# Between two MoE layers: where VectorE, ScalarE and TensorE each take a piece of the hand-over, in a three-stage attention and MoE kernel

## The chip, the cores and the metric

The kernel runs on one core of one Trainium2 chip. A time is the device time of that core in microseconds (us), from the first to the last instruction with what lies around it; of a kernel the median over several runs is given. A profile is of one further execution.

## What is computed

Attention over 4 batches, 8 heads, 768 positions and width 64, with a local window, a few global keys and a bias by distance; its output is read as 3072 tokens of width 512. Then two mixtures of eight experts (512 to 1024 to 512), the second on the output of the first:

```python
def _moe_ref(x, w_gate, w_output_gate, w1, w2):
    logits = x @ w_gate
    e_idx = np.argmax(logits, axis=1)
    ...
    for e in range(E):
        mask = e_idx == e
        h = np.maximum(x[mask] @ w1[e], 0.0)
        ye = h @ w2[e]
        out[mask] = gate_w[mask, None] * eom[mask, e, None] * ye

def _moe2_ref(x, w_gate, w1, w2):
    cap = N // E
    logits = x @ w_gate
    order = np.argsort(-logits.flatten())
    # greedy: each token goes to its best expert that has room, cap = 384 tokens each
    ...
    for e in range(E):
        mask = assigned == e
        h = np.maximum(x[mask] @ w1[e], 0.0)
        out[mask] = h @ w2[e]
```

The second assignment depends on all logits at once, so it can't begin before the first MoE has given the logits of every token.

## The kernel before

**Products in two parts.** Each fp32 matrix is split into a high part (the value rounded by ScalarE, names ending in h: wah, wbh, xh, hh) and a low part (the value less the high part: wal, wbl, xl, hl), and each product is three matmuls. `weight_chunk` (line 113) does this for a weight: a load of 512 KB into `raw` on the SP queue (three buffers, and one more for the last chunk later on), the high part on ScalarE (L119), the low part by a subtraction (L121) on the engine that `lo_engine` names, in one instruction or in two halves; `load_w1` and `load_w2` call it for the four chunks of a matrix. Layer 1 of an expert is at L175 with its evictions at L179 (ScalarE) and L180 (VectorE), layer 2 at L207, or L191 in transposed form.

**Two MoEs.** The loop over eight expert positions of the first MoE runs position e's layer 1 and layer 2 in turn, but of the last two (6 and 7) it runs layer 1 alone. Their logits for the second MoE are taken from the hidden rows at once (`gate_early` at L935, copied by ScalarE at L788 out of `lp` into a tile of name yo, turned by TensorE at L792, reduced by VectorE at L794, scattered by GpSimd at L86). So all logits are in DRAM before the last two layer 2 have run; the load of `L` (L1364, SP) collects them. Position 7's second matrix is loaded into the tag "wa", as soon as layer 1 of position 7 has read that tag for the last time.

**The second MoE** assigns one expert at a time: `phase(i, ...)` finds the expert that fills next by picking digits of the sorting key (six rounds; in each VectorE compares at L1123, TensorE counts at L1134, VectorE copies at L1136, TensorE folds at L1141, VectorE compares at L1144, TensorE spreads at L1150, VectorE takes the digit at L1152). Then L1216 and L1225 name the expert (`ei`, on which SP waits to load its first matrix, tag "wb"), L1229 to L1241 place its tokens (`cs`, `spx`, and the copy `csb` at L1234), and 24 matmuls at L1281 give their row numbers (`idx`, L1283 and L1285). GpSimd gathers these rows (L1321) into XB, TensorE turns them (L151), and the expert's layers follow.

**What sets the order.** TensorE's order is written out by `merge(ffns(), [phases(), weights(), tokens()])`: each matmul of the layers yields its modelled duration in ns (a 512-column one 213), each step of a phase yields how long to let the layers run before its next step, and `merge` interleaves them by these numbers. `ffns` begins with layer 2 of positions 6 and 7 (192 matmuls at L207, with `out1` as what is done with each of their eight row blocks, L946 and a scatter at L86); only phase 0 runs beside them, the phases from 1 on wait for their end. Phase 0 begins after 10000 ns of them. The other engines' orders come from a scheduler that simulates the program. Each engine works through its order strictly, so a wait holds everything behind it.

Of the kernel before, what the change touches and what calls it, by code (L numbers as in the profile page):

```python
# [14 lines left out]
AF = mybir.ActivationFunctionType  # L15
OP = mybir.AluOpType
# [13 lines left out]
def attention_moe_moe_kernel(  # L30
# [17 lines left out]
    nc = tc.nc  # L48
# [36 lines left out]
    def scatter(kind, dst, idx, src):  # L85
        st = nc.gpsimd.indirect_dma_start(  # L86
            out=dst, out_offset=bass.IndirectOffsetOnAxis(ap=idx, axis=0), in_=src, in_offset=None)
        indep(kind, st)
        return st
# [23 lines left out]
    def weight_chunk(src, tag, i, nfree, lo_engine, raw_view, halves=False):  # L113
        rp, nb_ = (raw_pools[-1], 1) if i == 3 and len(raw_pools) > 1 else (raw_pools[0], 3)
        raw = rp.tile([128, nfree], F32, tag="raw", name="raw", bufs=nb_)
        nc.sync.dma_start(raw if raw_view is None else raw.rearrange(raw_view[0], **raw_view[1]), src)
        hi = wpool.tile([128, nfree], F32R, tag=f"{tag}h{i}", name=f"{tag}h{i}")
        lo = wpool.tile([128, nfree], F32R, tag=f"{tag}l{i}", name=f"{tag}l{i}")
        nc.scalar.activation(hi, raw, AF.Copy)  # L119
        for c in (slice(0, nfree // 2), slice(nfree // 2, nfree)) if halves else (slice(0, nfree),):  # L120
            lo_engine.tensor_tensor(lo[:, c], raw[:, c], hi[:, c], op=OP.subtract)  # L121
        return hi, lo

    def load_w1(src, tag="wa", lo=(nc.gpsimd,), ks=range(KD), halves=False):
        return [weight_chunk(src[kk], tag, kk, FF, lo[kk % len(lo)], None, halves) for kk in ks]

    def load_w2(src, tag="wb", ks=range(KF // 2), lo_engine=nc.gpsimd, halves=False):
        r = []
        for i in ks:
            hi, lo = weight_chunk(src[i], tag, i, 2 * DM, lo_engine, ("p (c d) -> p c d", dict(c=2)), halves)  # L130
            for c in range(2):
                r.append((hi[:, c * DM:(c + 1) * DM], lo[:, c * DM:(c + 1) * DM]))
        return r
# [122 lines left out]
    with ExitStack() as actx:  # L256
# [68 lines left out]
        if not dense:  # L325
# [11 lines left out]
            if n_global:  # L337
                nc.vector.memset(dist[:, G0:G0 + n_global], float(n_local))
                nc.vector.tensor_scalar(dist[:, 256:256 + n_global], dist[:, 256:256 + n_global], float(n_local), None,
                                        op0=OP.min)  # L340
# [361 lines left out]
    def merge(main, sides):  # L702


        sides = [[s, 0.0] for s in sides]
        for cost in main:
            dt = max(0.0, min(w for _, w in sides)) if cost is None else cost
            for s in list(sides):
                s[1] -= dt
                while s[1] <= 0:  # L710
                    w = next(s[0], None)
                    if w is None:
                        sides.remove(s)
                        break
                    s[1] = w
        for s, _ in sides:
            for _ in s:
                pass
# [14 lines left out]
    def expert(i):  # L733

        if i not in who:
            who[i] = nc.sync.value_load(order[0:1, i:i + 1], min_val=0, max_val=E - 1)
        return who[i]

    def w1_of(i):
        return [w1[ds(expert(i), 1), kk * 128:(kk + 1) * 128].rearrange("o p f -> (o p) f") for kk in range(KD)]  # L740

    def w2_of(i):
        return [w2[ds(expert(i), 1), c * 256:(c + 1) * 256].rearrange("o (c p) d -> p (o c) d", p=128)
                for c in range(KF // 2)]
# [25 lines left out]
    with ExitStack() as bctx:  # L770
# [168 lines left out]
        def out1(e):  # L939
            sc, ii = aux[e]  # L940
            bt = PLAN[e][1]

            def done(j, yp):
                y = yb.tile([128, DM], F32, name="yo")[0:bt]
                with tc.high_priority():
                    nc.vector.tensor_scalar(y, yp, sc[:, j:j + 1], None, op0=OP.mult)  # L946
                    scatter("x2", x2d, ii[:, j:j + 1], y)
            return done

        last_load = [load_x(0)]  # L950
        last = [None]
# [14 lines left out]
        wa, wb = pre[0], pre[1]  # L966
# [3 lines left out]
        for e in range(E):  # L970
            hs = []
            nb, bt = PLAN[e]
            n_ = nb * bt
            l1 = layer1(wa, xt, n_, hs, e in (0 if dense else E, E - 1))
            mparts = [chain(*[gate_part(*p) for p in parts[e]])]
            if e == E - 2:
                merge(l1, mparts)
                lp = ps.tile([128, 512], F32, name="lp", tag="sp")[:, 0:n_]
                rest = chain(l2, gate_early(e, hs, mfs[e], lp))
            else:  # L980
                merge(l1, back + (mparts if e == E - 3 else []))
            if e + 1 < E:
                wa = load_w1(w1_of(e + 1), lo=(nc.gpsimd, nc.vector))
                xt = new_xt()

            def transposes(xt=xt, e=e, step=1500):
                for j in range(PLAN[e + 1][0]):
                    transpose_block(xt, XB[0:PLAN[e + 1][1], j], j, PLAN[e + 1][1])
                    yield step
                keep_aux(e + 1)  # L990

            if e < E - 2:
                yt = new_yt()
                l2 = layer2t(wb, hs, n_, yt)
                merge(islice(l2, 3 * KF * (KD - 1)) if e == E - 3 else l2, [transposes()] + (mparts if e < E - 3 else []))
                back = [rows_back(e, yt)]
                last_load[0] = load_x(e + 2)
                if e < E - 3:
                    wb = load_w2(w2_of(e + 1))
            elif e == E - 2:  # L1000
                merge(rest, [transposes(step=1200)])
                back.append(gate_scatter(lp, nb, bt, *aux[e], wait=5000))
                wb = load_w2(w2_of(e))
                hs_last.append((hs, wb))
            else:
                lp = ps.tile([128, 512], F32, name="lp", tag="sp")[:, 0:n_]
                for _ in gate_early(e, hs, mfs[e], lp):
                    pass
                for _ in gate_scatter(lp, nb, bt, *aux[e]):
                    pass  # L1010
                with tc.issue_after(last[0].ins):
                    wb = load_w2(w2_of(e), tag="wa")
                hs_last.append((hs, wb))


# [64 lines left out]
    def phase(i, found):  # L1080

        last = i == E - 1
# [15 lines left out]
        else:  # L1098
# [8 lines left out]
            y = sel.tile([128, 6, NC_], F32, name="yk")  # L1107
# [96 lines left out]
            for i_ in range(2):  # L1204
# [4 lines left out]
                                           op0=OP.is_ge, op1=OP.mult)  # L1209
# [14 lines left out]
        ei = sel.tile([128, 1], I32, name="ei", bufs=E)  # L1224
        nc.vector.tensor_scalar(ei, mx, -1.0, float(E), op0=OP.mult, op1=OP.add)  # L1225
        found.append(ei)
        yield 700
        cs = ps.tile([128, 1], F32, name="cs", tag="sp")
        nc.tensor.matmul(cs, stz, ones[:, 0:1], start=True, stop=True)  # L1229
        sp = ps.tile([128, 2, NC_], F32, name="spx", tag="sp")  # L1230
# [59 lines left out]
    w1t, w2s, xts, done1 = {}, {}, {}, set()  # L1290

    def phases():
        yield 10000
        for i in range(E):
            while i and -2 not in done1:
                yield 100
            for w in phase(i, found[i]):
                yield (1.04 if i else 0.9) * w
# [98 lines left out]
```

## Time and profile before

| what | value |
|---|---|
| time, median of 3 runs | 992.79 us (989.91 to 995.12) |
| the profiled execution's own time | 986.66 us |
| its span, first to last instruction | 984.9 us |
| TensorE busy | 927.5 us, 94% of the span |
| VectorE, ScalarE, GpSimd busy | 556.2, 424.5, 298.5 us |
| mean granted clock of TensorE | 0.979 of full speed |

The profile gives for each engine what it did and what ended the idle time before it. TensorE is busy nearly throughout, so what matters are the places where it stands still or runs at the lower of its two clock levels (1.2 in place of 2.4 GHz); a busy share doesn't show the second, the granted clock does. The stretch between the two MoEs lies at 565 to 650 us of the span, the last phase at 885 to 905 us.

### The profile page before, as it was taken

To read this page: it belongs to the slowest core of one execution; us is meant where nothing else is said; L and a number is where in the kernel's file an instruction comes from. 1 tells how busy PE (TensorE), PEld (TensorE's weight loads), DVE (VectorE), ACT (ScalarE), POOL (GpSimd) and SP (SyncE) were. 2 spreads that over 40 slices of the span, in tenths; PEclk is the share of its full clock that TensorE was granted. 3 is DMA by queue.
4 is the path that set the end of the run, shared out by engine and by line. 5 is a ranking of instruction groups with operands and counts; after the bars stand their busy time and mean duration, and the time that the engine had idled before them with its cause. 6 is when DMAs were issued, how large, how long until landed. Compare 5 with 4: busy or idle time off the path is not lost.

```text
span 984.9 us, 17460 instructions
## 1 busy us (share of the span) xinstructions
PE 927.5 (94%) x6253; PEld 773.4 (79%) x6253; DVE 556.2 (56%) x1928; ACT 424.5 (43%) x939; POOL 298.5 (30%) x272
## 2 busy tenths in 40 slices
PE   7999999999987999999999989689999999998997
PEld 6877777776886899899797756587868787787996
DVE  6657676676232443433334345877878688784530
ACT  5887878875233433334234320134333333432430
POOL 3111534241135465463623871301020210103001
PEclk9999999999998999999999999889999999998999
DMA  8999855630364446544441411515244261524510
GB/s 162 203 200 198 209 140 140 135 124 33 97 195 168 147 134 203 154 141 126 143 150 65 129 52 42 207 51 204 97 150 150 87 213 48 201 101 165 177 39 32
DMA packets 124192, 133.24 MB, mean 135 GB/s; under 512 B 83445, under 2 KB 83585, under 8 KB 124097
## 3 DMA queue, kind: packets, MB, share of 16 engines
q1 hardware_dynamic: 114449, 105.96, 38.6%
q0 software_dynamic: 9648, 26.09, 8.2%
q8 instruction: 51, 0.84, 0.4%
q14 instruction: 44, 0.36, 0.1%
HBM read 103.77 MB, written 28.23 MB: 134 GB/s over the span
## 4 chain that ended last, share of the span: by engine, by line
PE 47%; DVE 8%; issue 7%; DMA 5%; POOL 3%; ACT 1%; POOLq 0%; ACTq 0%; SPq 0%; DVEq 0%
PE hp L175 21%; PE yp L207 12%; PE yp L191 7%; DMA raw<-in_moe_w_dram 4%; DVE wal L121 4%; PE hp L151 2%; PE ip L1281 1%; POOL lg_dram L86 1%; POOL wbl L121 1%; PE cg L1134 1%; DVE geT L1123 1%; DMA XB<-x_dram,idx 1%; ACT wah L119 1%; DVE wbl L121 1%; POOL out_dram L86 1%
## 5 line engine op out<-in xcount | busy, mean ns | idle before, releaser
L179 ACT ACTIVATE hh<-hp 128x384 fp32r<-128x384 f32 (+9 forms) x130 | 63.4, 489 | 186.8 <-PE hp L175 173.1
L180 DVE SCALAR_TENSOR_TENSOR hl<-hp,hh 128x384 fp32r<-128x384 f32 (+9 forms) x130 | 71.8, 554 | 112.5 <-ACT hh L179 112.1
L86 POOL DMA_INDIRECT out_dram<-yo,idx x24 | 26.2, 1091 | 255.1 <-ACT yo L1359 227.1
L121 POOL TENSOR_TENSOR wbl<-raw,wbh 128x1024 fp32r<-128x1024 f32 x28 | 66.4, 2388 | 95.8 <-ACT wbh L119 55.8
L458 ACT ACTIVATE pb<-pb,mn 128x232 f32<-128x232 f32 (+1 forms) x192 | 88.8, 465 | 15.1 <-DVE mn L456 14.5
L207 PE MATMUL yp<-wah,hh 128*128 128x512 f32 x224 | 93.0, 415 | 0.0
L121 DVE TENSOR_TENSOR wal<-raw,wah 128x512 fp32r<-128x512 f32 (+1 forms) x78 | 67.4, 903 | 45.0 <-ACT wah L119 44.5
L119 ACT ACTIVATE wbh<-raw 128x1024 fp32r<-128x1024 f32 x60 | 62.7, 1058 | 69.1 <-DMA raw<-in_moe_w_dram 64.8
L207 PE MATMUL yp<-wah,hl 128*128 128x512 f32 x224 | 91.8, 410 | 0.0
L207 PE MATMUL yp<-wal,hh 128*128 128x512 f32 x224 | 91.4, 408 | 0.0
L444 PE MATMUL sc<-kx,qd 128*128 128x232 f32 (+1 forms) x384 | 88.7, 355 | 2.5 <-POOL kx L420 1.3
L175 PE MATMUL hp<-xl,wah 128*128 128x240 f32 (+8 forms) x260 | 90.9, 349 | 0.0
L175 PE MATMUL hp<-xh,wah 128*128 128x240 f32 (+8 forms) x260 | 90.1, 346 | 0.4 <-PEq L835 0.4
L175 PE MATMUL hp<-xh,wbh 128*128 128x384 f32 (+1 forms) x260 | 90.0, 346 | 0.0
L175 PE MATMUL hp<-xh,wal 128*128 128x240 f32 (+8 forms) x260 | 89.8, 346 | 0.0
L119 ACT ACTIVATE wah<-raw 128x1024 fp32r<-128x1024 f32 x68 | 68.6, 1052 | 48.4 <-DMA raw<-in_moe_w_dram 46.9
L175 PE MATMUL hp<-xh,wbl 128*128 128x384 f32 (+1 forms) x260 | 89.4, 344 | 0.0
L175 PE MATMUL hp<-xl,wbh 128*128 128x384 f32 (+1 forms) x260 | 89.4, 344 | 0.0
L456 DVE CUSTOM_DVE_ANT_0 pb<-sc,bias_w 128x232 f32<-128x232 f32 x160 | 56.7, 393 | 32.3 <-PE sc L444 18.5
L444 PEld LDWEIGHTS sc<-kx,qd 128*128 128x128 f32 x384 | 64.3, 194 | 10.1 <-POOL kx L420 2.4
L121 POOL TENSOR_TENSOR wal<-raw,wah 128x1024 fp32r<-128x1024 f32 x22 | 58.2, 2658 | 42.2 <-ACT wah L119 27.1
L191 PE MATMUL yp<-hh,wbh 128*128 128x240 f32 (+5 forms) x192 | 65.5, 341 | 3.1 <-ACT yt L197 2.1
(307 smaller groups left out, 2140.7 us busy)
## 6 DMA issues: line engine op xcount, KB each, us to landing
raw<-in_moe_w_dram SPq DMA_DIRECT2D x128, 512.0 KB
xs_dram<-qd SPq DMA_DIRECT2D x8, 1032.0 KB
vn<-in_v_dram SPq DMA_DIRECT2D x32, 192.0 KB
kn<-in_k_dram SPq DMA_DIRECT2D x30, 192.0 KB
qn<-in_q_dram SPq DMA_DIRECT2D x30, 192.0 KB
rawg<-in_moe_w_dram SPq DMA_DIRECT2D x8, 512.0 KB
XB<-xs_dram SPq DMA_DIRECT2D x9, 241.9 KB
XB<-xs_dram SPq DMA_DIRECT2D x7, 258.0 KB
```

What stands on the lines that cost most here:

```text
L86: st = nc.gpsimd.indirect_dma_start(out=dst, out_offset=bass.IndirectOffsetOnAxis(ap=idx, axis=0), in_=src, in_offset=None)
L119: nc.scalar.activation(hi, raw, AF.Copy)
L121: lo_engine.tensor_tensor(lo[:, c], raw[:, c], hi[:, c], op=OP.subtract)
L151: tr = nc.tensor.transpose(tp[:, kk], rows[:, kk * 128:(kk + 1) * 128], ident[0:nt, 0:nt])
L175: nc.tensor.matmul(hp_[:, :m], a[:, c], b_[:, kk, t], start=(i == 0), stop=(i == 3 * KD - 1))
L179: nc.scalar.activation(hh[:, t], hp_[:, :m], AF.Relu)
L180: nc.vector.scalar_tensor_tensor(hl[:, t], hp_[:, :m], 0.0, hh[:, t], op0=OP.max, op1=OP.subtract)
L191: nc.tensor.matmul(yp, a[:, c], b_[:, :n], start=(f == 0 and i == 0), stop=(f == KF - 1 and i == 2))
L207: last_mm[0] = nc.tensor.matmul(yp, a[:, c], b_, start=(f == 0 and i == 0), stop=(f == KF - 1 and i == 2))
L444: nc.tensor.matmul(sc[:, h, off:], lhs, kx[:, t, off:], start=True, stop=True)
L456: nc.vector.tensor_tensor_reduce(p[:, h, off:], sc[:, h, off:], bt, 1.0, 3.0e38, OP.add, OP.min, mn)
L458: nc.scalar.activation(p[:, h, off:], p[:, h, off:], AF.Exp, bias=mn, scale=-1.0, accum_out=sums[:, t, hh:hh + 1])
```

## The change

Four edits, three of them in the stretch between the MoEs:

- the low parts of position 7's second matrix are made by VectorE in halves (before: by GpSimd, whole chunks);
- the eight row blocks of the last two layer 2 are scaled by ScalarE (before: by VectorE);
- phase 0 begins after 14500 ns of the last two layer 2 (before: 10000);
- in the last phase (i = 7) the step from the naming of the expert to `cs` and `spx` is 4000 ns (before: 700; a factor of 1.04 comes on top).

```diff
@@ -943,7 +943,7 @@
             def done(j, yp):
                 y = yb.tile([128, DM], F32, name="yo")[0:bt]
                 with tc.high_priority():
-                    nc.vector.tensor_scalar(y, yp, sc[:, j:j + 1], None, op0=OP.mult)
+                    nc.scalar.activation(y, yp, AF.Copy, scale=sc[:, j:j + 1])
                     scatter("x2", x2d, ii[:, j:j + 1], y)
             return done
@@ -1009,7 +1009,7 @@
                 with tc.issue_after(last[0].ins):
-                    wb = load_w2(w2_of(e), tag="wa")
+                    wb = load_w2(w2_of(e), tag="wa", lo_engine=nc.vector, halves=True)
                 hs_last.append((hs, wb))
@@ -1224,7 +1224,7 @@
         found.append(ei)
-        yield 700
+        yield 4000 if last else 700
         cs = ps.tile([128, 1], F32, name="cs", tag="sp")
@@ -1290,7 +1290,7 @@
     def phases():
-        yield 10000
+        yield 14500
         for i in range(E):
```

**ScalarE, at the end of layer 1 of position 7** (wah0 to wah3 are the high parts of position 7's second matrix, yo<-lp the copy of its logits). Before:

```order
L119 ACTIVATE wah2_7619<-raw_7617 128x1024
L179 ACTIVATE hh7_7557<-hp_7559 128x512
L788 ACTIVATE yo_7591<-lp_7574 128x512
L119 ACTIVATE wah3_7625<-raw_7623 128x1024
L119 ACTIVATE wbh0_8062<-raw_8060 128x1024
```

Now:

```order
L119 ACTIVATE wah2_7621<-raw_7619 128x1024
L179 ACTIVATE hh7_7557<-hp_7559 128x512
L119 ACTIVATE wah3_7628<-raw_7626 128x1024
L788 ACTIVATE yo_7591<-lp_7574 128x512
L946 ACTIVATE yo_7714<-yp_7689,sc_7021 120x512
...
L946 ACTIVATE yo_8113<-yp_8007,sc_7317 128x512
L119 ACTIVATE wbh0_8087<-raw_8085 128x1024
L946 ACTIVATE yo_8183<-yp_8116,sc_7317 128x512
L119 ACTIVATE wbh1_8094<-raw_8092 128x1024
```

The conversion of the fourth chunk, wah3, moved ahead of the logits' copy; the eight scalings are new here, the last of them behind wbh0, the first chunk of the second MoE's first expert.

**VectorE, where the rows of expert 0 are found** (wbl0 to wbl3 are the low parts of that expert's first matrix, idx its row numbers, cgz the first copy of phase 1). Before:

```order
L946 TENSOR_SCALAR yo_8151<-yp_8031,sc_7317 128x512
...
L121 TENSOR_TENSOR wbl2_8077<-raw_8074,wbh2_8076 128x512 x2
L1165 CAST kf_8221<-ki_8220 128x120
L121 TENSOR_TENSOR wbl3_8084<-raw_8081,wbh3_8083 128x512 x2
L946 TENSOR_SCALAR yo_8208<-yp_8154,sc_7317 128x512
L1285 SCALAR_TENSOR_TENSOR idx_8193<-ip_8166,icp_8191 128x3
L1136 CAST cgz_7667<-cg_8248 128x2x8
```

Now:

```order
L121 TENSOR_TENSOR wbl2_8102<-raw_8099,wbh2_8101 128x512 x2
L1165 CAST kf_8225<-ki_8224 128x120
L121 TENSOR_TENSOR wbl3_8109<-raw_8106,wbh3_8108 128x512 x2
L1136 CAST cgz_7671<-cg_8252 128x2x8
L1285 SCALAR_TENSOR_TENSOR idx_8213<-ip_8186,icp_8211 128x3
```

The two last scalings are gone from this piece; cgz and idx both stay behind all four low parts. On TensorE the whole of phase 0 moved 21 of the 512-column matmuls back: its first count (L1134) stands behind 82 of them in place of 61, and the 24 matmuls of L1281, which had 13 of them behind, now follow the last one.

**TensorE, in the last phase** (cs and spx place expert 7's tokens). Before:

```order
L207 MATMUL yp_11532<-wah1_11273,hl2_11353 128x512
L207 MATMUL yp_11532<-wah1_11273,hh3_11377 128x512
L1229 LDWEIGHTS stz_7673
L1229 MATMUL cs_11629<-ones_75,stz_7673 128x1
L1232 LDWEIGHTS before_73
L1232 MATMUL spx_11631<-stz_7673,before_73 128x48
```

Now:

```order
L207 MATMUL yp_11650<-wah0_11270,hh0_11296 128x512
L207 MATMUL yp_11650<-wal0_11271,hh0_11296 128x512
L1229 LDWEIGHTS stz_7677
L1229 MATMUL cs_11653<-ones_75,stz_7677 128x1
L1232 LDWEIGHTS before_73
L1232 MATMUL spx_11655<-stz_7677,before_73 128x48
```

Both moved 16 matmuls back, from the fifth matmul after the L1281 group of phase 6 to the twenty-first. On VectorE csb and phase 6's idx changed places behind the last low part, idx now first.

## Rows read from the trace of the kernel before

**Rows 1.** Windows: us; busy us (and instructions) of PE, PEld, DVE, ACT, POOL; PEclk; DMA share; GB/s

```profile
415.00:420.00 5.00, 5.00 (x25) 4.97 (x24) 2.30 (x7) 0.00 (x0) 0.00 (x0) 0.71 0.39 127
...
890.00:895.00 5.00, 5.00 (x13) 3.61 (x14) 2.88 (x12) 0.00 (x0) 2.90 (x3) 0.50 0.83 288
```

**Rows 2.** Timeline of PE: start us, us, what, count, [idle before <- what ended it]

```profile
573.13 0.66 PE L792 MATMUL hp<-ident,yo 128*128 128x128 f32 x4 [0.84 <-ACT yo L788]
...
592.13 0.49 PE L1134 MATMUL cg<-ohb,geT 128*128 128x16 bf16 x12 [4.26 <-DVE geT L1123]
...
595.43 0.20 PE L1150 MATMUL fp<-flz,onesb 128*128 128x64 bf16 x1
...
605.31 0.46 PE L1134 MATMUL cg<-ohb,geT 128*128 128x16 bf16 x12
...
607.27 0.20 PE L1150 MATMUL fp<-flz,onesb 128*128 128x64 bf16 x1
```

**Rows 3.** Timeline of DVE, start of phase 0

```profile
582.99 3.63 DVE L1110 TENSOR_SCALAR ki<-vmax 128x24 int32<-128x24 int32 x1
...
587.10 3.10 DVE L1114 TENSOR_SCALAR ki<-ki 128x24 int32<-128x24 int32 x1
```

**Rows 4.** Timeline of POOL: low parts, scatters of rows, first gather

```profile
579.46 7.12 POOL L121 TENSOR_TENSOR wal<-raw,wah 128x1024 fp32r<-128x1024 f32 x3
...
626.00 3.92 POOL L86 DMA_INDIRECT x_dram<-yo,ii  x1 [7.00 <-DVE ki L1163]
632.62 0.97 POOL L86 DMA_INDIRECT x_dram<-yo,ii  x1 [2.70 <-DVE cgz L1136]
638.11 0.99 POOL L1321 DMA_INDIRECT XB<-x_dram,idx  x1 [4.52 <-DVE cgz L1136]
```

**Rows 5.** Timeline of ACT, from the end of layer 1 of position 7

```profile
566.51 2.95 ACT L119 ACTIVATE wah<-raw 128x1024 fp32r<-128x1024 f32 x3
...
572.48 0.60 ACT L788 ACTIVATE yo<-lp 128x512 f32<-128x512 f32 x1 [2.54 <-issue]
585.77 1.06 ACT L119 ACTIVATE wah<-raw 128x1024 fp32r<-128x1024 f32 x1 [12.69 <-DMA raw<-in_moe_w_dram]
623.30 1.06 ACT L119 ACTIVATE wbh<-raw 128x1024 fp32r<-128x1024 f32 x1 [36.48 <-DMA raw<-in_moe_w_dram]
```

**Rows 6.** Timeline of PE, end of the last layer 2 to layer 1 of expert 0

```profile
619.16 0.20 PE L1241 MATMUL spx<-before,csb 128*128 128x48 f16 x1
...
625.35 1.82 PE L1281 MATMUL ip<-br,slots 128*128 128x6 f16 x24
...
629.91 0.40 PE L207 MATMUL yp<-wah,hl 128*128 128x512 f32 x1
...
638.28 0.18 PE L1150 MATMUL fp<-flz,onesb 128*128 128x32 bf16 x1 [0.33 <-DVE flz L1144]
641.54 1.11 PE L151 MATMUL hp<-ident,XB 128*128 128x128 f32 x4 [3.08 <-DMA XB<-x_dram,idx]
...
645.57 0.51 PE L175 MATMUL hp<-xh,wbh 128*128 128x192 f32 x1
```

**Rows 7.** Timeline of DVE, the low parts of expert 0's first matrix

```profile
624.98 0.74 DVE L946 TENSOR_SCALAR yo<-yp,sc 128x512 f32<-128x512 f32 x1
...
630.41 1.28 DVE L121 TENSOR_TENSOR wbl<-raw,wbh 128x512 fp32r<-128x512 f32 x2
...
632.34 0.15 DVE L1136 CAST cgz<-cg 128x16 f16<-128x16 f32 x1
```

**Rows 8.** Timeline of PE, the last phase, and the fourteenth L207 matmul after it

```profile
889.73 0.20 PE L1232 MATMUL spx<-stz,before 128*128 128x48 f16 x1 [2.67 <-DVE csb L1234]
...
895.69 0.44 PE L207 MATMUL yp<-wah,hl 128*128 128x512 f32 x1
```

**Rows 9.** Timeline of PE, two other idle times of about 2 us

```profile
413.73 0.44 PE L191 MATMUL yp<-hh,wbh 128*128 128x384 f32 x1 [2.12 <-ACT yt L197]
...
486.86 0.64 PE L917 MATMUL mp<-wt,wg2p 128*32 128x256 f32 x8 [2.20 <-DVE wt L913]
```

## The prediction

> **What bounds the kernel now.** I read the page's busy shares first: TensorE works 94% of the span, so a gain has to come from its idle times and from stretches at its lower clock. The list of what TensorE waited for, and then its timeline, show three such places near the edits. First, the first count of phase 0 stands in front of the remaining matmuls for 4.26 us, until VectorE's geT is there [rows 2]. Second, between the last matmul of position 7 at 629.91 and the first turned rows of expert 0 at 641.54 only small steps of phase 1 run [rows 6]. Third, in the last phase spx waits 2.67 us [rows 8]. The windows show the granted clock at 0.50 after that last wait [rows 1]: the engine stood still, and what follows runs at 1.2 GHz for a while. All else in the span I take as unmoved, since the order of instructions outside these places is the same.
>
> **The change, part by part**, against the profiled execution (986.66 us of its own; the median of the runs, 992.79, is 6.13 above it, and I carry that distance over).
>
> *Low parts to VectorE, and phase 0's start.* Phase 0's first steps on VectorE take 3.63 and 3.10 us for two tiny integer operations [rows 3]; a copy of that size takes 0.15 [rows 7]. The reason is beside them: GpSimd's three subtractions run from 579.46 for 7.12 us, to 586.58 [rows 4], and VectorE's first operation ends at 582.99 + 3.63 = 586.62. With GpSimd free, some 6.4 us of these 6.7 go. *The Trainium skill (SBUF — State Buffer, "Who interferes with whom") says that VectorE and GpSimd share one port pair as an exclusive lock, held for a whole instruction; the two ends 0.04 us apart agree.* Besides, phase 0 stands 21 matmuls later on TensorE. A matmul takes 0.233 us: 26 of them and two small groups lie between 619.16 and 625.35 [rows 6]. That is 4.9 us of slack. Either edit alone covers the 4.26 us; together I take the stall as gone with about 6 us to spare: **-4.26**. The half-clock tail behind it goes too: from the count to the spread of that round 592.13 to 595.43 = 3.30 us, the same piece at full clock 605.31 to 607.27 = 1.96 [rows 2]: **-1.34**.
>
> *What is late next.* ScalarE's order puts wah3 ahead of the logits' copy, and that copy holds TensorE at L792. Before, the fourth chunk came at 585.77, long after the copy at 572.48 [rows 5], because its buffer came free only when GpSimd had subtracted the first chunk (579.46 plus a third of 7.12, 581.8): 3.9 us for release, load and landing. Now VectorE subtracts the first chunk from 567.5 (a third of 2.95 after 566.51 [rows 5]) in 1.28 us [rows 7], to 568.8; plus 3.9 is 572.7; wah3 takes 1.06, so the copy starts at 573.7, 1.2 us later than before. **+1.2** on TensorE, whose idle time there grows from 0.84 to 2.1 us. Bounds: 0 if the load is faster than the one that had another load beside it, 2.5 if it lands 1.3 later. Of two such idle times elsewhere, 2.12 and 2.20 us [rows 9], the first was followed by a window at 0.71 of the clock [rows 1], the second not (its eight matmuls ran at once in 0.64). I leave the tail out of the sum and keep 1.3 us for the range.
>
> VectorE's order now has six subtractions ahead of hl7, which comes some 2 us later, still before the copy above could start; free. The logits' scatters, and so L, come 1.2 us later: inside the 6 us to spare.
>
> *The end of the last layer 2.* L1281's group, 1.82 us long [rows 6] with its last 0.15 beside the next matmul, moves behind the last matmul: 1.67 us leave the path of the rows. The last matmul starts at 629.91 - 4.26 - 1.34 - 1.67 + 1.2 = 623.8, and layer 2 ends at 624.1, 6.1 earlier. What the rows of expert 0 need isn't that alone. L1241 has 18 matmuls behind it in place of 39 with the L1281 group, so it runs at about 619.8, not earlier than before (619.16). From it hangs a chain on VectorE: placing the tokens, then the four low parts wbl0 to wbl3 (1.28 us each), then cgz, the first copy of phase 1. That took 632.34 - 619.16 = 13.2 us [rows 6, 7] with two scalings in it; these leave VectorE, about 0.7 us each (0.74 [rows 7]), which makes 11.8: cgz at 631.6, only 0.7 earlier. On TensorE three rounds of phase 1 stand ahead of the turned rows, 638.28 - 632.34 = 5.9 us after cgz: 637.6, and the turning starts at 637.8. Before, it waited for the gathered rows until 641.54, so **the turning starts 3.7 earlier, not 6.1**. In return the fourth round of phase 1 is no longer ready when the first rows are turned; before, turning to layer 1 took 645.57 - 641.54 = 4.03 us, and I add 0.5. Layer 1 of expert 0 starts **3.2 us earlier** than 645.57. This 3.2 contains all of the terms above.
>
> *Scaling on ScalarE.* ScalarE stood idle for 36.48 us ahead of wbh0 [rows 5], so seven of eight are free (an activation of this size, the logits' copy, takes 0.60). The last one stands behind wbh0, which I place 0.6 later than its 623.30, as L1241 is, and ending at 625.0; its scatter starts at 625.8. That scatter then lies beside VectorE's subtractions. Such a one took 3.92 us at 626.00, a free one 0.97 [rows 4]. I take 3.92, the row it is nearest to: end at 629.7. The gather started 4.52 after the last scatter's end [rows 4] and its rows were there 3.43 later (641.54 - 638.11): 637.7. That is level with the 637.8 above; no cost.
>
> *The last phase.* cs and spx stand 16 matmuls back, 3.7 us, and the wait was 2.67: **-2.67**. Behind it 14 matmuls, the first at once and the last at 895.69, ran mostly at half clock: 13 steps in 5.93 us, where 13 x 0.233 plus 0.15 for the small ones is 3.18 [rows 8]: **-2.75**. What spx may really have waited for, its buffer, is freed by phase 6's idx, which now comes first. Phase 7's later row numbers cost nothing: its rows are turned some 20 us on.
>
> **Sum**: -3.2 - 5.4 = -8.6 us; 978.1 for the profiled execution, **984.2** for the median.
>
> **The rivals.** (a) *The rows bind the gap, not the rounds.* If expert 0's weights land sooner, or the copy isn't held, the whole 6.1 (7.3 without the 1.2) comes through: -11.5 to -12.7, **980.1 to 981.3**. For it: before, the rows were the last to come. Against: cgz would have to run within 4 us of the end of layer 2, and the order puts four subtractions ahead. 0.15.
>
> (b) *The last scatter is held by VectorE's subtractions to their end.* Then it starts at 631.6 and ends at 632.6; the gather follows 4.52 later, the turning 3.43 after that, at 640.6; layer 1 4.03 later, 644.6, only 0.9 earlier: -6.3, **986.5**. For it: the 3.92. Against: there the scatter did end before the subtractions had. *The Trainium skill (SBUF — State Buffer, the box on the "DVE blocks DMA" trap) warns that GpSimd can't write a DMA's descriptors while VectorE holds the shared port; it speaks against putting more on VectorE here, and the 3.92 beside 0.97 agrees in kind.* 0.15.
>
> (c) *One of the two gains fails.* If another wait takes the place of spx's, -3.2 is left, 989.6; if the gap takes back all, -5.4, 987.4. For it: the gap had a hidden second limit already. 0.15.
>
> (d) *Slower: the fourth chunk comes as late as before.* TensorE stands at L792 until wah3 is done. If the buffer of the first chunk is freed as late as in rows 5, the copy starts at 586.8 in place of 573.7: 13.1 us more than forecast, plus a half-clock tail of 1.3 to 2.7: -8.6 + 15 = +6, **999**. The change decides for slower once the chunk lands 8.6 us after my 572.7, at 581. Against: VectorE has 2 us idle where its subtractions go, and nothing else asks for the buffer. 0.05.
>
> **How the numbers follow.** My forecast, with the 1.3 us of clock and the bounds of the load, spans 982.5 to 986 and has 0.50. A measurement of this kernel can tell about 0.5% from no change, 5.0 us: faster means below 987.8. Faster: 0.50 + 0.15 + 0.13 of (b) = 0.78. Same: most of (c) and the rest of (b) = 0.17. Slower: (d), 0.05. The range goes from (a) to the better-known half of (c): 979.8 to 990.0.
>
> **What would show it.** Right: no idle time above 0.5 us before the first L1134; L1110 of phase 0 below 0.4 us; an idle time near 2 us before L792; layer 2's end near 624 and the first L151 near 637.8, ended by phase 1's rounds and not by the gather; no wait before the last spx and clock 1.00 in the windows after it. Wrong: an L1281 or idx later than cgz by microseconds, an L151 that waits for XB beyond 639, a wait of spx or L1241 on csb, or a new stall in phases 1 to 6, whose orders I took as unmoved.

## The result, and the profile after

| | before | after |
|---|---|---|
| median | 992.32 us (12 runs, 989.65 to 998.03) | 983.32 us (12 runs, 979.49 to 989.35) |
| ratio | | 0.9915, 95% interval 0.9892 to 0.9939 |
| the profiled execution's own time | 986.66 us | 983.57 us |
| its span | 984.9 us | 981.8 us |

The change saves 9.0 us by the medians, 6.1 to 10.7 by the interval. The two profiled executions differ by 3.1 us only: the one of before lay 5.7 us under its median, and the one of after reached the last logits' product (first L935) 3.84 us later than it, in a part of the program whose orders the change leaves alone. From L935 to the end of the span the profile of before took 416.25 us and that of after 409.31. Times below are therefore counted from L935 or from L792, and where two profiles are compared closely, piece by piece.

TensorE's timeline of the kernel after, from the logits to layer 1 of expert 0 and in the last phase (start and duration in us, engine, line, operation, count, idle time before it and what ended that):

```profile
577.54 1.04 PE L935 MATMUL lp<-hl,mf 128*32 128x512 f32 x2 [0.89 <-DVE hl L180]
579.96 0.66 PE L792 MATMUL hp<-ident,yo 128*128 128x128 f32 x4 [1.37 <-ACT yo L788]
...
599.44 0.46 PE L1134 MATMUL cg<-ohb,geT 128*128 128x16 bf16 x12
...
601.37 0.20 PE L1150 MATMUL fp<-flz,onesb 128*128 128x64 bf16 x1
...
624.84 0.20 PE L1241 MATMUL spx<-before,csb 128*128 128x48 f16 x1
...
628.93 0.40 PE L207 MATMUL yp<-wah,hl 128*128 128x512 f32 x1
...
630.29 1.84 PE L1281 MATMUL ip<-br,slots 128*128 128x6 f16 x24 [0.97 <-DVE br L1277]
...
637.82 0.28 PE L1141 MATMUL cp<-fold,cgz 128*128 128x64 f16 x2 [3.40 <-DVE idx L1285]
...
643.59 0.18 PE L1150 MATMUL fp<-flz,onesb 128*128 128x32 bf16 x1 [0.33 <-DVE flz L1144]
643.71 1.11 PE L151 MATMUL hp<-ident,XB 128*128 128x128 f32 x4
...
648.29 0.51 PE L175 MATMUL hp<-xh,wbh 128*128 128x192 f32 x1
...
893.13 0.18 PE L1232 MATMUL spx<-stz,before 128*128 128x48 f16 x1
```

The first count has no idle time in front of it (4.26 in [rows 2]), and from it to the spread of that round are 601.37 - 599.44 = 1.93 us (3.30 before). The first turned rows start right behind phase 1's third spread; before, they waited for the gathered rows [rows 6]. The last spx has no wait either (2.67 in [rows 8]). The idle time before L792 grew from 0.84 to 1.37 us, and 0.89 before the last logits' products, for hl, is new.

VectorE's timeline of the same kernel, with position 7's low parts, phase 0's start, expert 0's low parts, and phase 6's idx and csb in the last phase:

```profile
573.19 3.70 DVE L121 TENSOR_TENSOR wal<-raw,wah 128x512 fp32r<-128x512 f32 x6
...
589.97 0.18 DVE L1110 TENSOR_SCALAR ki<-vmax 128x24 int32<-128x24 int32 x1
...
590.62 0.17 DVE L1114 TENSOR_SCALAR ki<-ki 128x24 int32<-128x24 int32 x1
...
591.72 0.94 DVE L1123 TENSOR_TENSOR geT<-db,jt 128x1536 bf16<-128x1536 bf16 x1
...
623.77 0.15 DVE L1225 TENSOR_SCALAR ei<-mx 128x1 int32<-128x1 f32 x1
...
631.62 1.29 DVE L121 TENSOR_TENSOR wbl<-raw,wbh 128x512 fp32r<-128x512 f32 x2 [0.88 <-ACT wbh L119]
632.84 0.17 DVE L1163 TENSOR_SCALAR ki<-ki 128x24 int32<-128x24 int32 x1
632.91 0.95 DVE L1123 TENSOR_TENSOR geT<-db,jt 128x1536 bf16<-128x1536 bf16 x1
...
636.39 1.28 DVE L121 TENSOR_TENSOR wbl<-raw,wbh 128x512 fp32r<-128x512 f32 x2
637.60 0.16 DVE L1136 CAST cgz<-cg 128x16 f16<-128x16 f32 x1
...
891.01 0.15 DVE L1285 SCALAR_TENSOR_TENSOR idx<-ip,icp 128x3 int32<-128x3 f32 x1
893.32 0.29 DVE L1234 CAST csb<-cs 128x128 f16<-128x128 f32 x1 [2.16 <-PE cs L1229]
```

The two integer operations take 0.18 and 0.17 us where they took 3.63 and 3.10 [rows 3]. geT is there 6.8 us ahead of the count. The copy cgz runs after the fourth low part, as its place in the order says, and TensorE's 3.40 us before L1141 are the wait for it (the row's releaser, idx, is the operation after it).

ScalarE's timeline of the same kernel, with the conversions before the logits' copy and the last scaling:

```profile
572.10 2.95 ACT L119 ACTIVATE wah<-raw 128x1024 fp32r<-128x1024 f32 x3
...
578.37 1.06 ACT L119 ACTIVATE wah<-raw 128x1024 fp32r<-128x1024 f32 x1 [2.83 <-DMA raw<-in_moe_w_dram]
579.33 0.58 ACT L788 ACTIVATE yo<-lp 128x512 f32<-128x512 f32 x1
...
630.53 1.06 ACT L119 ACTIVATE wbh<-raw 128x1024 fp32r<-128x1024 f32 x1 [6.42 <-DMA raw<-in_moe_w_dram]
631.49 0.67 ACT L946 ACTIVATE yo<-yp,sc 128x512 f32<-128x512 f32 x1
```

The logits' copy waits for the fourth conversion, and that for its load. The last scaling stands behind wbh0. GpSimd's timeline, the last scatter and the first gather for expert 0:

```profile
632.44 1.32 POOL L86 DMA_INDIRECT x_dram<-yo,ii  x1 [7.09 <-ACT yo L946]
638.71 0.99 POOL L1321 DMA_INDIRECT XB<-x_dram,idx  x1 [4.95 <-DVE flz L1144]
```

Beside VectorE's subtractions the last scatter takes 1.32 us. The windows of the kernel after (window, its length, busy time and count of each engine, TensorE's granted clock, DMA share, GB/s) show the clock at its upper level, 2.4 GHz, where [rows 1] had 0.50 in the last phase:

```profile
890.00:895.00 5.00, 5.00 (x25) 3.68 (x25) 1.98 (x7) 0.60 (x1) 2.45 (x3) 1.00 0.90 304
895.00:900.00 5.00, 5.00 (x25) 4.09 (x24) 3.29 (x13) 1.20 (x2) 1.83 (x3) 1.00 0.61 229
```

### The profile page after: what moved, and what is told of

The parts are those of the page before. It is cut to its first block, busy times and chain, and to the rows that moved or that the text cites. A ratio compares the mean times of both kernels' runs of the same rounds, so it can differ in the third digit from the quotient of the medians.

```text
span 981.8 us, 17465 instructions
## 1 busy us (share of the span) xinstructions
PE 924.4 (94%) x6253; PEld 771.0 (79%) x6253; DVE 549.5 (56%) x1928; ACT 430.3 (44%) x947; POOL 287.0 (29%) x268
## 5 line engine op out<-in xcount | busy, mean ns | idle before, releaser
L121 DVE TENSOR_TENSOR wal<-raw,wah 128x512 fp32r<-128x512 f32 (+1 forms) x86 | 72.3, 881 | 45.9 <-ACT wah L119 45.5
L207 PE MATMUL yp<-wah,hh 128*128 128x512 f32 x224 | 92.5, 413 | 0.0
L207 PE MATMUL yp<-wah,hl 128*128 128x512 f32 x224 | 90.7, 405 | 0.0
L207 PE MATMUL yp<-wal,hh 128*128 128x512 f32 x224 | 90.1, 402 | 0.0
L191 PE MATMUL yp<-hl,wbh 128*128 128x240 f32 (+5 forms) x192 | 65.6, 342 | 0.1
```

The source lines that it names most:

```text
L191: nc.tensor.matmul(yp, a[:, c], b_[:, :n], start=(f == 0 and i == 0), stop=(f == KF - 1 and i == 2))
L207: last_mm[0] = nc.tensor.matmul(yp, a[:, c], b_, start=(f == 0 and i == 0), stop=(f == KF - 1 and i == 2))
```

## The experiments

Three sets of four kernels, each beside runs of the kernel before on the same chip (medians of before: 996.73, 985.09 and 991.05 us). Ratios are to those runs.

### One part at a time

**The last phase's sums alone.**

```diff
-        yield 700
+        yield 4000 if last else 700
```

> Kernel before with the last phase's longer step alone. My theory: the 2.67 us wait of the last spx and the half-clock stretch behind it (2.75) both go, nothing takes their place: about 5.4 us less, ratio near 0.9945, clock 1.00 in the windows after the last phase, first-count wait of phase 0 still near 4 us. Rival (another wait takes its place, on the copy csb or on the buffer): a wait of 1 us or more before spx or L1241, clock still 0.5 behind it, ratio 0.998 to 1.002.

990.16 us, ratio 0.9932 (0.9909 to 0.9954). TensorE's timeline of this run:

```profile
600.14 0.48 PE L1134 MATMUL cg<-ohb,geT 128*128 128x16 bf16 x12 [4.24 <-DVE geT L1123]
...
899.55 0.18 PE L1232 MATMUL spx<-stz,before 128*128 128x48 f16 x1
```

The wait of spx is gone and the other stall is where it was: this part gives 6.6 us by the medians, and the 5.4 of the forecast lie inside the interval (4.6 to 9.1).

**The low parts alone, in halves on VectorE.**

```diff
-                    wb = load_w2(w2_of(e), tag="wa")
+                    wb = load_w2(w2_of(e), tag="wa", lo_engine=nc.vector, halves=True)
```

> Kernel before with the low parts of position 7's second matrix on VectorE alone, phase 0 at its old place. My theory (GpSimd's subtractions held VectorE's tiny integer operations): L1110 and L1114 of phase 0 below 0.4 us each, the wait before the first count below 1 us and no half-clock stretch behind it; the copy of the logits waits for the fourth chunk, 1 to 3 us; in all 2.6 to 4.4 us less, ratio 0.9955 to 0.9975. Rival (the logits' late landing is what the count waits for): the wait stays at 3 us or more with short integer operations, ratio 1.000.

993.22 us, ratio 0.9960 (0.9943 to 0.9977). The count (605.14) has no wait, L1110 takes 0.18 us, L792 waits 1.48 us. So this part alone does cover the 4.26 us: layer 1 of expert 0 comes 76.04 us after L935, 79.38 in the run before this one.

**Phase 0's later start alone.**

```diff
-        yield 10000
+        yield 14500
```

> Kernel before with phase 0's later start alone. My theory: either edit covers the 4.26 us wait, so it goes here too although L1110 still takes about 3.6 us; but phase 0 names its expert later against the last layer 2, so the gap takes part of it back: layer 1 of expert 0 about 3 us earlier, ratio near 0.997. Rival (the wait needs the port to be free): a wait of 2 us or more before the first count, ratio 1.000 or above.

997.18 us, ratio 1.0005 (0.9989 to 1.0021): nothing. The theory fell. TensorE's timeline of this run:

```profile
581.27 0.66 PE L792 MATMUL hp<-ident,yo 128*128 128x128 f32 x4 [0.74 <-ACT yo L788]
...
601.09 0.49 PE L207 MATMUL yp<-wbh,hh 128*120 128x512 f32 x1 [2.50 <-DVE yo L946]
...
604.43 0.53 PE L1134 MATMUL cg<-ohb,geT 128*128 128x16 bf16 x12
```

VectorE's timeline of the same run, just ahead of that:

```profile
591.19 3.55 DVE L1110 TENSOR_SCALAR ki<-vmax 128x24 int32<-128x24 int32 x1
...
595.21 3.16 DVE L1114 TENSOR_SCALAR ki<-ki 128x24 int32<-128x24 int32 x1
...
599.29 0.95 DVE L1123 TENSOR_TENSOR geT<-db,jt 128x1536 bf16<-128x1536 bf16 x1
600.30 0.74 DVE L946 TENSOR_SCALAR yo<-yp,sc 120x512 f32<-120x512 f32 x1
```

The count itself does not wait any more, but a matmul of layer 2 ahead of it does: its buffer in PSUM, the memory that TensorE writes to, has to be emptied by a scaling, and that scaling is queued on VectorE behind the two held operations and geT. The wait moved from L1134 to L207, 2.50 us, and the granted clock of 602 to 606 was 0.57. The count comes 604.43 - 581.27 = 23.16 us after L792 where the kernel after needs 19.48, and layer 1 of expert 0 comes 78.85 us after L935, near the 79.38 of the run with the last phase alone.

**After, with the early start put back.**

```diff
-        yield 14500
+        yield 10000
```

> Changed kernel with phase 0's start put back to 10000. My theory (with the low parts on VectorE the later start isn't needed, and it costs in the gap): wait before the first count below 1 us; the first turned rows wait for the gather again, not for phase 1's rounds; 1 to 2.5 us faster than the changed kernel, ratio to before 0.989 to 0.991. Rival (the later start is what removes the wait): a wait of 2 us or more before the first count, 2 to 4 us slower than the changed kernel, ratio 0.994 to 0.996.

986.39 us, ratio 0.9903 (0.9884 to 0.9923). No wait before the count; so the later start isn't needed once VectorE has the low parts. Now the gathered rows end the wait before the turning (646.39, 4.05 us, the third spread had run at 642.16), which starts 69.84 us after L935 where the kernel after has 71.22.

### What the later start needed

**After, with the low parts left on GpSimd.**

```diff
-                    wb = load_w2(w2_of(e), tag="wa", lo_engine=nc.vector, halves=True)
+                    wb = load_w2(w2_of(e), tag="wa")
```

> The kernel after with its low parts back on GpSimd: phase 0 still starts 14500 ns in, ScalarE still scales, the last phase's sums still come late. In the run of the later start alone, a matmul of layer 2 waited 2.50 us for a scaling on VectorE that stood behind the held integer operations, and a half-clock stretch followed; the first count came 3.7 us later after L792 than in the kernel after. Theory: that scaling, not the count, was what the held operations still cost, so with the scalings on ScalarE the loss is gone although L1110 still takes over 3 us: no wait above 0.5 us of L207 between L792 and the first count, the count 19 to 20 us after L792 (23.2 in that run), and a ratio of 0.989 to 0.993. Rival: TensorE waits there for geT or another product of VectorE; then the 2.5 us and its tail stay, and only the last phase's gain and a little of the gap are left: 0.993 to 0.996.

974.88 us, ratio 0.9898 (0.9873 to 0.9923). TensorE's timeline of this run:

```profile
574.59 0.66 PE L792 MATMUL hp<-ident,yo 128*128 128x128 f32 x4 [0.84 <-ACT yo L788]
...
594.06 0.46 PE L1134 MATMUL cg<-ohb,geT 128*128 128x16 bf16 x12
...
638.86 1.12 PE L151 MATMUL hp<-ident,XB 128*128 128x128 f32 x4 [1.35 <-DMA XB<-x_dram,idx]
```

VectorE's timeline of it, two operations of phase 0:

```profile
584.46 3.63 DVE L1110 TENSOR_SCALAR ki<-vmax 128x24 int32<-128x24 int32 x1
...
592.65 0.95 DVE L1123 TENSOR_TENSOR geT<-db,jt 128x1536 bf16<-128x1536 bf16 x1
```

And GpSimd's, the subtractions beside them:

```profile
580.93 7.12 POOL L121 TENSOR_TENSOR wal<-raw,wah 128x1024 fp32r<-128x1024 f32 x3
```

VectorE is held as before, to 588.09, 0.04 us after GpSimd's end at 588.05. TensorE notices nothing: geT ends at 593.60, 0.46 us ahead of the count, which stands 19.47 us after L792. No L207 waits, since the scalings are ScalarE's. Theory right: to spare TensorE this stall, the later start needs the scalings off VectorE and nothing else. The turning was bound by the gathered rows here (1.35 us), not by the rounds.

**After, with the scalings back on VectorE.**

```diff
-                    nc.scalar.activation(y, yp, AF.Copy, scale=sc[:, j:j + 1])
+                    nc.vector.tensor_scalar(y, yp, sc[:, j:j + 1], None, op0=OP.mult)
```

> The kernel after with the scalings back on VectorE. Theory: with the low parts in halves on VectorE nothing holds it, so scaling there costs little: no wait of L207 for yo above 0.5 us, but the last scaling stands among the four low parts of expert 0 and so cgz, the rounds of phase 1 and the turning come 0.7 to 1.5 us later than in the kernel after: ratio 0.992 to 0.994 where the kernel after had 0.9915. Rival one: the scaling on ScalarE is needed for layer 2 in any case; then L207 waits again by over 1 us and the ratio is 0.995 or more. Rival two: it does nothing at all, 0.990 to 0.9915.

976.85 us, ratio 0.9920 (0.9897 to 0.9943). No L207 waits, the count comes 19.48 us after L792; cgz runs 631.04 - 617.93 = 13.11 us after L1241 where the kernel after needs 12.76. From L792 to layer 1 of expert 0 it took 69.26 us, against 68.33 and 67.70 in the two profiles of the kernel after: beside low parts on VectorE the scaling is worth some 0.9 to 1.6 us there, about as expected. The ratio, whose interval holds all three forecasts, doesn't tell.

**The scalings on ScalarE and the last phase's edit, nothing else** (the kernel before with these two).

```diff
-                    nc.vector.tensor_scalar(y, yp, sc[:, j:j + 1], None, op0=OP.mult)
+                    nc.scalar.activation(y, yp, AF.Copy, scale=sc[:, j:j + 1])
...
-        yield 700
+        yield 4000 if last else 700
```

> The kernel before with the scalings on ScalarE and the last phase's sums late; low parts on GpSimd, phase 0 starts 10000 ns in. Theory: with this start the first count stands 4.9 us of matmuls earlier, geT is held by GpSimd's subtractions as before, so the 4.26 us wait and its half-clock tail stay: an idle time of 4 to 4.6 us before the first count, ratio 0.992 to 0.9945, that is the last phase's gain alone (0.9932 measured) and at most 1 us from the scalings. Rival: the scalings on VectorE were what made geT late; then the wait falls below 2 us and the ratio is below 0.991.

In the third set: 986.30 us, ratio 0.9947 (0.9925 to 0.9968); the wait before the count is 4.27 us, with 0.54 of the clock from 599 to 605. The scaling alone gives nothing there, as expected: the three parts for the first stall are not alike. The low parts remove the hold; the later start passes it by, if the scalings are off VectorE.

### What the low parts cost

**The logits' copy ahead of the conversions**, with the early and with the later start.

```diff
-            nc.scalar.activation(lt, lp, AF.Copy)
+            last[1:] = [nc.scalar.activation(lt, lp, AF.Copy)]
...
-                with tc.issue_after(last[0].ins):
+                with tc.issue_after(last[0].ins), tc.issue_after(last[1].ins):
```

> The kernel after with phase 0 again starting 10000 ns in, and with ScalarE's order changed at one place: the last hidden rows and the logits' copy ahead of the four conversions of the last weight, which were made ahead of them before. Theory: in the kernel after, the copy stood behind the fourth conversion, and TensorE idled 1.37 us before L792 and 0.89 us before the last logits' matmul; now both idle times fall to 0.8 and below 0.3, layer 2 ends 1.5 to 2 us earlier after L935, and because the gathered rows end the wait for the first turned rows with this start (L151 waited 4.05 us for them, three rounds of phase 1 were done by then), the turning comes as much earlier: ratio 0.987 to 0.9895, where 10000 with the old order had 0.9903. Rival: the conversions, now later, make layer 2 wait for the last weight's chunks, and nothing is gained: 0.990 or more, with a wait on wah or wal.

> The kernel after with only that change of ScalarE's order (phase 0 starts 14500 ns in). Theory: L792 again 1.5 to 2 us earlier after L935, and the rounds of phase 1, which end the wait here, move with it, since phase 0's steps are interleaved at the same matmuls: ratio 0.989 to 0.990, 1 to 1.5 us above the run with the earlier start, whose turning is not held by the rounds. Rival: the start of phase 0 does not matter by a microsecond: the same ratio as that run to 0.0005.

Early 975.09 us, 0.9904 (0.9879 to 0.9930); later 975.46 us, 0.9901 (0.9876 to 0.9925). The idle time before L792 is 0.84 us in both and L792 comes 4.48 and 4.49 us after L935 (7.47 in the kernel after), no matmul waits for a conversion. The first expectation named a ratio of 0.987 to 0.9895 and missed it with 0.9904, though the interval reaches down to 0.9879. The early start lost part of its lead because geT is now 1.04 us late for the count: from L792 to the turning it took 63.49 us, and 62.16 with the early start and the old order. The last matmul of layer 2 comes 56.43 us after L935, 53.47 with the later start; most of the rest of that difference is the group of L1281, which with the early start stands ahead of it. The turning starts 67.97 and 67.51 us after L935, layer 1 of expert 0 72.00 and 71.89: with the early start the rows end the wait (3.09 us), with the later one phase 1's rounds do. That is the rival of the second expectation: with the copy first, the start doesn't matter in the traces. The two ratios agree, but their intervals are too wide to tell a microsecond. Start early and the rows are late; start late and the rounds are.

**All in one set.** After, after with the low parts left on GpSimd, and after with the copy first were run once more side by side.

> The kernel after once more, beside the next three on the same chip, for a direct comparison. Its ratio was 0.9915 with 0.9892 to 0.9939; 0.990 to 0.993 is expected. Theory: the first matmul at L792 comes 6.0 to 7.5 us after the last logits' product begins (4.5 where the copy isn't held), no wait of the first count, no wait of spx.

> The kernel after with its low parts back on GpSimd, once more, beside the kernel after. Theory: the move of the low parts to VectorE saves nothing once ScalarE scales and phase 0 starts late (the count came 0.46 us after geT was there), and it costs the held copy at L792, 1.5 to 3 us: this run is 1 to 3 us faster than the kernel after of the same set, ratio 0.988 to 0.991. Rival: the low parts on VectorE are worth something elsewhere (the scatters behind the subtractions on GpSimd, the rows): this run is as slow as the kernel after or slower.

> The kernel after with the logits' copy ahead of the conversions on ScalarE, once more, beside the kernel after. Theory: L792 comes 4.5 us after the last logits' product begins and everything behind it moves along, the turning included: 1.5 to 3 us faster than the kernel after of the same set, ratio 0.988 to 0.991, and level within 1 us with the low parts left on GpSimd. Rival: the conversions, which now run later, or the rows take the gain back; then it is level with the kernel after within 0.5 us.

| kernel | median | ratio to before | L935 to L792 | L935 to layer 1 of expert 0 |
|---|---|---|---|---|
| after | 984.68 us (12 runs) | 0.9939 (0.9917 to 0.9962) | 7.40 us | 75.10 us |
| low parts left on GpSimd | 980.67 us (6 runs) | 0.9895 (0.9862 to 0.9928) | 5.69 us | 73.99 us |
| copy first | 981.39 us (6 runs) | 0.9899 (0.9865 to 0.9934) | 4.48 us | 71.86 us |

TensorE's timeline of after in this set:

```profile
577.08 0.66 PE L792 MATMUL hp<-ident,yo 128*128 128x128 f32 x4 [1.74 <-ACT yo L788]
```

And of the run with the low parts left on GpSimd:

```profile
577.10 0.66 PE L792 MATMUL hp<-ident,yo 128*128 128x128 f32 x4 [0.74 <-ACT yo L788]
...
596.57 0.46 PE L1134 MATMUL cg<-ohb,geT 128*128 128x16 bf16 x12
```

Both versions came out faster than the kernel after, by 4.0 and 3.3 us of the median, somewhat more than expected; after itself lay just above its expected 0.990 to 0.993. Their intervals overlap that of after at the edge. Taken against after itself, the means of the set's runs differ by 4.0 us (95% interval 1.7 to 6.4) and 3.4 (0.7 to 6.1): that both are faster is clear of noise, the size isn't settled. The traces show 1.1 and 3.2 us of it up to layer 1 of expert 0. What is shown is the place: with the low parts on VectorE the logits' copy stands behind a fourth conversion that it need not wait for, 7.40 - 5.69 = 1.7 us, and 6.06 - 4.49 = 1.6 between the run with the scalings back and the one with the low parts left in the second set. The run with the low parts left on GpSimd does without one of the change's four edits, and had 0.9898 and 0.9895 in its two sets.

## Why the prediction was right, and where it wasn't

The forecast was 984.2 us, and 983.32 was measured. Its sum, -8.6, stands against -9.0 by the medians of the result and -6.4 in the third set of the experiments (991.05 to 984.68). So the closeness of the first is in part luck. In the third set the two edits of the first stall, low parts and later start, come to 1.6 us by the medians (986.30 to 984.68); in its traces they come to 4.2 up to layer 1 of expert 0 (79.31 and 75.10 after L935). Medians of twelve runs don't settle a term of this size; the steps below go by the traces:

- **"Either edit alone covers the 4.26 us": wrong for the later start.** The run of it alone gained nothing. The arithmetic for the count was right: 4.9 us of slack against 4.26 left 0.64, and 0.46 was measured with the low parts left on GpSimd. What the step left out is who else is queued behind the held operations: the scaling L946, and behind it a PSUM buffer that layer 2 needs. With both edits in, it made no difference to the sum.
- **-4.26 and -1.34 for stall and tail: right.** No wait; 1.93 us from count to spread, forecast 1.96.
- **+1.2 for the held copy: right mechanism, somewhat too small (1.6 to 1.7).** The copy starts 579.33 - 572.10 = 7.23 us after the first conversion, forecast 573.7 - 566.51 = 7.19; the fourth chunk's conversion starts 3.95 us after the first chunk's subtraction ended (573.19 plus a third of 3.70), forecast 3.9. What the step took as fixed is the start of the conversions themselves: 2.14 us ahead of L935 in the profile of before, 0.39 and 0.82 ahead in the two of after. With the order of before, too, L792 comes 4.48 us after L935 after an early start of them, 5.65 to 5.80 after a late one. Between profiles that start alike the hold cost 1.6 and 1.7 us. The 0.89 us for hl cost nothing more, as forecast, since the copy still waited for the conversion. No clock tail followed (1.00 from 580 to 590), as the sum had it.
- **cgz 11.8 us after L1241: 12.76 and 12.12 in the profiles of after, 11.84 and 11.80 in two runs beside.** The chain is the named one. Its length goes with the landing of expert 0's chunks: the first was converted 6.76 and 6.12 us after ei in the profiles of after and 5.85 and 5.73 in the two beside, where the step took the 5.14 of before. The later chunks count as well: in the second run with the low parts left the first came after 5.81, the others late, and the chain took 12.72.
- **The turning is bound by phase 1's rounds, not by the rows: right.** From cgz to the turning 6.11 us (6.2 forecast), from there to layer 1 4.58 (4.53). It was close, as the forecast had it: in two of the eight profiles with the later start the rows ended the wait, by 1.35 and 0.36 us.
- **Layer 1 of expert 0 3.2 us earlier: about right.** After L935 it comes at 76.92 in the profile of before and at 75.80 and 75.10 in those of after, which is only 1.1 and 1.8 less; but in that of before the conversions began early. Against the run with only the last phase changed, where they began as late as in the kernel after, it is 3.6 and 4.3 less (79.38). From L792 to layer 1 the kernel after took 68.33 and 67.70 us, before 72.44, and 73.60 in the run with only the last phase changed. That is 4.1 to 5.9 less, and 1.7 back for the copy: 2.4 to 4.2.
- **Scaling on ScalarE and the last scatter: no cost, right**, though the scatter took 1.32 us and not 3.92. An activation takes 0.67 to 0.69, not 0.60.
- **The last phase, -5.4: right.** From layer 1 of expert 0 to the end of the span: 339.33 us before, 338.47 and 337.98 in the two runs without this edit, 333.15 to 333.81 in ten of the eleven profiles with it, 335.32 in the other. In the kernel after spx ran at 893.13, ahead of csb (893.32). So csb, which [rows 8] name as what ended the wait, isn't what spx needs; it had stood ahead of phase 6's idx there. idx ran at 891.01 now, which fits the buffer that the prediction suspected.

Of the rivals, (a) would have needed the rows to bind; in both profiles of after the rounds did. (b) took the subtractions for one stretch to their end; in the kernel after their halves came in pairs, and the scatter ended 0.85 us after the first pair. *The Trainium skill (SBUF — State Buffer, the box on the "DVE blocks DMA" trap) warns of descriptors that GpSimd can't write while VectorE runs an operation in a 2-port mode; VectorE's operations here are subtractions of two operands in SBUF, and the rows agree in kind: the scatter took 1.32 us in the profile of after, 0.97 alone, and one took 3.95 in the run with the early start, at the row block before.* (c) needed one gain to fail; both came. (d) needed the fourth chunk 8.6 us later than forecast; it came as forecast.

What the experiments don't settle: whether the later start by itself helps or harms beside low parts on VectorE (0.9903 without it, 0.9915 and 0.9939 with it, in different sets; in the traces layer 1 of expert 0 comes 73.88 us after L935 without it, 75.80 and 75.10 with it), and why the part before L935, whose orders are the same, takes some microseconds more in one execution than in another.

## What to carry to other kernels

When an engine is held, list everything that is queued behind the held instruction, not only the one result that the stall names: moving its consumer later only hands the wait to the next in the queue, here a PSUM buffer that waited to be emptied. Two edits that each look sufficient on paper should be tried alone; here one was sufficient, the other only together with a third, and that pair made the first, the only edit with a price, unnecessary. And work moved to a faster engine frees a buffer earlier, which pulls a load and a conversion ahead of something that others wait for: look at what the scheduler now puts in front.

## What was unexpected on the chip

- The length of a scatter beside VectorE's subtractions can't be taken over from one row. The 3.92 us of [rows 4] belong to the last row block but one, the 1.32 above to the last, which took 0.97 before. Both ended 0.85 us after an operation of VectorE on two operands in SBUF. In the kernel before that was geT, behind four halves without a gap (629.07 and 629.92); in the kernel after it was the first pair of subtractions (632.91 and 633.76), behind which stands an operation on one operand, L1163. VectorE's timeline of the kernel before:

```profile
625.72 2.49 DVE L121 TENSOR_TENSOR wbl<-raw,wbh 128x512 fp32r<-128x512 f32 x4
628.13 0.94 DVE L1123 TENSOR_TENSOR geT<-db,jt 128x1536 bf16<-128x1536 bf16 x1
```

  And GpSimd's of the run with the early start, again the last block but one, beside four subtractions and a geT that ended at 633.52:

```profile
630.56 3.95 POOL L86 DMA_INDIRECT x_dram<-yo,ii  x1 [6.20 <-ACT yo L946]
```

  That a hold lasts to the end of such a stretch isn't shown: in the run with the copy first and the early start, a scatter of 1.17 us ended at 574.17 inside subtractions from 572.63 to 575.12.
- The start of the same three conversions on ScalarE lay 2.13 or 2.14 us ahead of L935 in three of the profiles with the same order there and 0.25 to 0.82 in the other eight. What delays them is not shown. One profile of before is a thin base for a term of 1 us.
- The hold of VectorE ended 0.04 us after GpSimd's subtractions in the run with the low parts left as well (588.09 against 588.05), as in [rows 3, 4]. *The Trainium skill (SBUF — State Buffer, "Who interferes with whom") calls this an exclusive lock for the length of an instruction; these rows agree on the hold: two instructions of 0.18 and 0.17 us became 3.63 and 3.17.* It lasted longer than one instruction of GpSimd: VectorE's first operation began at 584.46, in the second of three subtractions of 2.4 us each, and ended only with the third.
